# Reordering the early stage of a chunked-scan and gated-FFN kernel: weight groups of two, earlier loads, the decay matmul moved, D in two parts

## The chip, the cores and the metric

The kernel runs on one core of one Trainium2 chip. The metric is device time in us. A profiled execution gives a trace, with a span from its first to its last instruction; the span is some 1.7 to 2.0 us shorter than the time. Engines: TensorE (PE, its weight loads PEld), VectorE (DVE), ScalarE (ACT), GpSimd (POOL), SyncE (SP, which issues most of the DMAs here). In this kernel matmul results go to banks of PSUM, and another engine copies them out ("evacuates" them).

## The reference

```python
# x (4, 8, 768, 32), a (4, 8, 768), B and C (4, 8, 768, 16), float32
for each chunk of 32 tokens:                      # the kernel uses chunks of 64 or 128
    M = (C @ B^T) * decay(i, j) * causal          # C @ B^T is "G" in the kernel
    y = M @ x + (C @ state) * decay_to_i          # "D" and "inter" in the kernel
    state = decay_full * state + sum_j B x decay  # "state sums" (adds, carry, pass_on)
t = y as (3072, 256)
out = (relu(t @ w_gate) * (t @ w_val)) @ w_out    # 256 -> 1536 -> 256
```

## The kernel before

Batch 0 is worked off in pairs of 256 tokens (pairs 0 to 2), the FFN in blocks of 512 tokens. Each engine gets its instructions in the order of the program. From pair 3 on the scan is woven into the FFN, and that part is not changed. The pieces that matter:

```python
def keep_warm(n, tag="shared"):          # "dummies": results are never read
    ...
    for _ in range(n):
        nc.tensor.matmul(out=w, lhsT=warm, rhs=warm, start=True, stop=True)   # 128x128x128 bf16

def decay():                             # fp32, 64 rows; HC = 3, six records in the trace
    for k in range(HC):
        nc.tensor.matmul(out=d[:, k]..., lhsT=cp[:, k * 128:(k + 1) * 128], rhs=pick...)

def D_wide(p):                           # 32 small matmuls
    for t in range(2):
        for r in range(2):
            for i in range(2):
                ...
                for q in range(4):       # q: head group = column group of the array
                    nc.tensor.matmul(out=y[32 * q:32 * q + 32, t], lhsT=..., rhs=...,
                                     tile_position=(64 * i, 32 * q), ...)
...
keep_warm(20)
d = factors(); decays(0); decays(1)      # fp32 matmuls
keep_warm(3)
...
weights(0, 4)                            # GpSimd DMA, w_gate and w_val, four 128-column tiles each
...
scan(0, H)
scale_wide(1, 1, P_); weights(4, 8); scale_wide(1, 0, P_)      # pair 1, on GpSimd
keep_warm(4)
G_wide(0)
keep_warm(16)
...
cast_x(0, A_); adds(0)                   # state sums of pair 0
keep_warm(3)
...
pass_on(0, 0); carry(0, 0); middle(); inter_wide(0); D_wide(0)
turn(1, True); yevac_wide(0, A_, V); ...
f0 = gvh(0, 0, 0, True)                  # FFN, one tile of 128 columns, 256 tokens ("a half")
G_wide(1)
decay()
...
```

## Time and profile before

| | before |
|---|---|
| time, median of the first 3 runs | 130.36 us (130.0 to 130.37) |
| span of the profiled run | 129.2 us (a fourth run, time 130.95 us) |
| TensorE busy | 121.2 us, 94% |
| TensorE alone on the chain of waits | from 35.1 us on, but for the last copy (0.42 us) |
| holes of TensorE before that | 0.54 (at 10.96), 0.55 (15.55), 1.47 (25.28) |

"Busy" is the time in which an instruction's record runs. The profile's rows and timelines are shown in the prediction.

### The profile page before, as it was taken

What the parts mean: (1) busy time and instruction counts of PE and PEld (TensorE: products, weight loads), DVE (VectorE), ACT (ScalarE), POOL (GpSimd) and SP (SyncE); (2) the same over time, 40 slices, a digit from 0 to 9 for tenths busy, and PEclk for the clock granted to TensorE, in tenths of its full rate; (3) what the DMA queues carried; (4) which work ended last, traced back from release to release, by engine and by line L of the source; (5) the groups of instructions that cost most, each with busy time, mean ns of one, the idle gap of its engine ahead of it and who ended that gap; (6) DMA issues with size and microseconds to landing.
All of it is one profiled execution on the core that took longest, in us unless ns stands there. A gap on an engine that the chain in (4) does not pass through costs nothing.

```text
span 129.2 us, 3445 instructions
## 1 busy us (share of the span) xinstructions
PE 121.2 (94%) x1288; PEld 84.5 (65%) x1294; DVE 88.5 (68%) x201; ACT 81.7 (63%) x186; POOL 40.2 (31%) x84
## 2 busy tenths in 40 slices
PE   6998899599999999999999999999999999999990
PEld 6764577258677567784567875477864577854770
DVE  4895968436599966578675878765789675688410
ACT  0567579355588854787844797935887745876310
POOL 6558402477285003480003760011930033000000
PEclk9999999999999999999999999999999999999999
DMA  4999999998889987288841188932200002200031
GB/s 71 208 152 186 173 210 196 122 121 100 100 101 215 105 110 90 86 143 108 99 61 66 41 139 98 103 49 89 81 0 0 0 5 81 81 0 5 0 110 52
DMA packets 72208, 12.14 MB, mean 94 GB/s; under 512 B 65936, under 2 KB 72192, under 8 KB 72192
## 3 DMA queue, kind: packets, MB, share of 16 engines
q1 hardware_dynamic: 66096, 8.91, 44.2%
q0 software_dynamic: 3184, 2.36, 13.0%
q10 hardware_dynamic: 2912, 0.66, 2.4%
q8 instruction: 10, 0.16, 0.6%
q14 instruction: 6, 0.05, 0.1%
HBM read 11.13 MB, written 3.15 MB: 110 GB/s over the span
## 4 chain that ended last, share of the span: by engine, by line
PE 82%; DMA 9%; DVE 2%; issue 2%; ACT 2%; POOL 0%; SPq 0%; DVEq 0%; POOLq 0%; ACTq 0%
PE o L604 24%; PE gv L586 15%; PE val L571 13%; PE gate L568 12%; DMA bcr<-in_B_dram 9%; PE w L184 4%; PE y L543 2%; PE tp L325 2%; PE g L469 2%; PE A_ps L506 1%; PE y L532 1%; PE g L362 1%; DVE h L575 1%; PE tpb L325 1%; ACT CT L343 1%
## 5 line engine op out<-in xcount | busy, mean ns | idle before, releaser
L575 DVE TENSOR_TENSOR h<-r,val 128x512 bf16<-128x512 bf16 x42 | 28.3, 685 | 9.9 <-ACT r L574 8.9
L604 PE MATMUL o<-wo,h 128*128 128x256 bf16 x288 | 34.8, 273 | 0.1
L604 PEld LDWEIGHTS <-h 128*128 128x128 bf16 x288 | 27.4, 98 | 5.5 <-issue 1.3
L574 ACT ACTIVATE r<-gate 128x512 bf16<-128x512 f32 x42 | 24.6, 601 | 6.4 <-PE gate L568 5.0
L592 DVE TENSOR_TENSOR h<-r,gv 128x256 bf16<-128x256 bf16 x60 | 23.7, 419 | 7.0 <-ACT r L589 6.6
L477 POOL TENSOR_SCALAR_AFFINE_SELECT gs<-gs 128x512 bf16<-128x512 bf16 (+1 forms) x18 | 9.0, 523 | 52.5 <-ACT gs L488 52.5
L571 PE MATMUL val<-yT,wv 128*128 128x512 bf16 x84 | 25.0, 379 | 0.3
L589 ACT ACTIVATE r<-gv 128x256 bf16<-128x256 f32 x60 | 22.6, 384 | 3.6 <-PE gv L586 1.7
L568 PE MATMUL gate<-yT,wg 128*128 128x512 bf16 x78 | 23.7, 379 | 0.0
L586 PE MATMUL gv<-yT,wv 128*128 128x256 bf16 x120 | 22.9, 273 | 0.6 <-DMA wv<-in_moe_w_val_dram 0.5
L586 PE MATMUL gv<-yT,wg 128*128 128x256 bf16 x120 | 23.0, 273 | 0.2
L494 DVE TENSOR_TENSOR gs<-g,maskUT 128x512 bf16<-128x512 f32 x18 | 11.6, 686 | 10.4 <-issue 9.7
L571 PEld LDWEIGHTS <-wv 128*128 128x128 bf16 x84 | 8.2, 98 | 9.9
L586 PEld LDWEIGHTS <-wv 128*128 128x128 bf16 x120 | 11.6, 98 | 2.5 <-DMA wv<-in_moe_w_val_dram 1.2
L586 PEld LDWEIGHTS <-wg 128*128 128x128 bf16 x120 | 11.1, 98 | 2.3 <-issue 0.5
L568 PEld LDWEIGHTS <-wg 128*128 128x128 bf16 x84 | 7.8, 98 | 5.8
L295 POOL TENSOR_TENSOR bs<-bcr,scaleBC 128x256 bf16<-128x256 f32 x18 | 11.0, 633 | 0.7 <-DMA bcr<-in_C_dram 0.7
L488 ACT CAST gs<-g 128x512 bf16<-128x512 f32 x9 | 5.3, 589 | 7.0 <-PE g L469 7.0
L620 ACT COPY ob<-o 128x512 f32<-128x512 f32 x10 | 5.8, 584 | 4.7 <-PE o L604 4.7
L556 ACT CAST yT<-y 128x512 bf16<-128x512 f32 x9 | 5.3, 586 | 5.5 <-PE y L543 5.3
L184 PE MATMUL w<-warm 128*128 128x128 bf16 x49 | 6.2, 308 | 1.1 <-DVE tmask L155 1.1
L325 PEld LDWEIGHTS <-bs 128*128 128x128 bf16 x48 | 3.5, 99 | 5.1 <-POOL bs L281 2.3
(100 smaller groups left out, 119.4 us busy)
## 6 DMA issues: line engine op xcount, KB each, us to landing
out_dram<-ob SPq DMA_DIRECT2D x10, 256.0 KB, 2.2
xr<-in_x_dram SPq DMA_DIRECT2D x19, 128.0 KB, 3.6
bcr<-in_C_dram SPq DMA_DIRECT2D x19, 64.0 KB, 3.3
bcr<-in_B_dram SPq DMA_DIRECT2D x19, 64.0 KB, 3.4
wg<-in_moe_w_gate_dram POOLq DMA_DIRECT2D x3, 256.0 KB, 5.6
wv<-in_moe_w_val_dram POOLq DMA_DIRECT2D x3, 256.0 KB, 6.1
wo<-in_moe_w_out_dram POOLq DMA_DIRECT2D x1, 768.0 KB, 11.6
xr<-in_x_dram SPq DMA_DIRECT2D x2, 256.0 KB, 8.6
```

The lines of the kernel that those rows point to most:

```text
L184: nc.tensor.matmul(out=w, lhsT=warm, rhs=warm, start=True, stop=True)
L295: eng.tensor_tensor(out=bs.rearrange("s k (q t n) -> s k t q n", q=4, t=2)[:, :, t], in0=src[:, :, t], in1=f[:, :, 4 * t:4 * t + 4].to_bro ...
L477: nc.gpsimd.affine_select(out=dst, in_=dst, pattern=[[0, n], [1, 128]], compare_op=ALU.is_ge, fill=0.0, base=0, channel_multiplier=-1)
L494: nc.vector.tensor_tensor(out=d[:, q], in0=g[q], in1=m, op=ALU.mult)
L568: nc.tensor.matmul(out=g, lhsT=wg[:, k, fs], rhs=yT[:, k, tk], start=(k == 0), stop=(k == 1))
L571: nc.tensor.matmul(out=v, lhsT=wv[:, k, fs], rhs=yT[:, k, tk], start=(k == 0), stop=(k == 1))
L574: nc.scalar.activation(r, g, AF.Relu)
L575: nc.vector.tensor_tensor(out=fst[b][:, f], in0=r, in1=v, op=ALU.mult)
L586: nc.tensor.matmul(out=gv_[:, j], lhsT=w[:, k, fs], rhs=yT[:, k, tk], start=(k == 0), stop=(k == 1), skip_group_check=True)
L589: nc.scalar.activation(r, gv_[:, 0], AF.Relu)
L592: nc.vector.tensor_tensor(out=fst[b][:, f, u * 256:(u + 1) * 256], in0=r, in1=gv_[:, 1], op=ALU.mult)
L604: nc.tensor.matmul(out=o[:, ts % 2], lhsT=fst[b][:, f, ts * 128:(ts + 1) * 128], rhs=wo[:, f], start=(f == 0), stop=(f == NF - 1), skip_gr ...
```

## The change

The intent is to close the three holes and to get the decay matmul out of real work. Weights come in groups of two tiles; loads of pairs 1 and 2 are let go sooner; w_out comes in two halves, the second later; the decay matmul takes the place of dummies; D is split by head group so that only one group waits for the last mask; pair 1's evacuation comes sooner; one output copy is split over two engines.

```diff
-        nc.vector.tensor_scalar_mul(pick[:, 0], pairs[:, 0], rmid)
+        nc.gpsimd.tensor_scalar_mul(pick[:, 0], pairs[:, 0], rmid)
...
-    def D_wide(p):
+    def D_wide(p, qs=(0, 1, 2, 3)):
...
+        if b == 0 and ts == 3:
+            nc.scalar.copy(out=ob[:, 0], in_=fst["o"][:, 0])
+            nc.vector.tensor_copy(ob[:, 1], fst["o"][:, 1])
...
-    weights(0, 4)
+    weights(0, 2)
+    weights(2, 4)
...
     scan(0, H)
+    middle()
     scale_wide(1, 1, P_)
-    weights(4, 8)
+    weights(4, 6)
     scale_wide(1, 0, P_)
+    weights(6, 8)
     keep_warm(4)
     G_wide(0)
-    keep_warm(16)
+    keep_warm(7)
+    load_x(1, nc.sync)
...
+    decay()
+    keep_warm(3)
     cast_x(0, A_)
     adds(0)
-    keep_warm(3)
...
+    decay_factors()
     pass_on(0, 0)
     carry(0, 0)
-    middle()
+    D_wide(0, (2, 3, 0))
     inter_wide(0)
-    D_wide(0)
+    D_wide(0, (1,))
     turn(1, True)
     yevac_wide(0, A_, V)
+    load(2)
+    load(3)
     carry(0, 1)
+    cast_x(1, P_)
     weights(8, NF)
-    cast_x(1, P_)
-    weights_out(0, NF)
+    weights_out(0, NF // 2)
...                                   (pair 1: adds, carry, pass_on, D and yevac sooner,
...                                    FFN halves 4 and 5 after them; weights_out(NF // 2, NF)
...                                    after scale_wide(2, 1))
+    halves(0, 1, 0, 1, 2, 3)
+    halves(0, 0, 6, 7)
+    halves(0, 1, 4, 5, 6, 7)
     gv(0, 8)
+    carry(1, 1)
+    pass_on(1, 1)
```

More of the change, by code (lines that the diff above doesn't have):

```diff
@@ L448, in D_wide @@
                     y = s["yw"][i][:, 0:256].rearrange("s (t m) -> s t m", t=2)
-                    for q in range(4):
+                    for q in qs:
                         nc.tensor.matmul(
@@ L619, in foevac @@
             return
-        nc.scalar.copy(out=ob, in_=fst["o"])
+        if b == 0 and ts == 3:
+            nc.scalar.copy(out=ob[:, 0], in_=fst["o"][:, 0])
+            nc.vector.tensor_copy(ob[:, 1], fst["o"][:, 1])
+        else:
+            nc.scalar.copy(out=ob, in_=fst["o"])
         nc.sync.dma_start(
@@ L647 @@
     scan(0, H)
+    middle()
     scale_wide(1, 1, P_)
-    weights(4, 8)
+    weights(4, 6)
     scale_wide(1, 0, P_)
+    weights(6, 8)
     keep_warm(4)
     G_wide(0)
-    keep_warm(16)
+    keep_warm(7)
+    load_x(1, nc.sync)
     gcopy(0, 0)
     gmask(0, 2, V, True)
-    load_x(1, nc.sync)
     gcopy(0, 1)
+    decay()
+    keep_warm(3)
     cast_x(0, A_)
     adds(0)
-    keep_warm(3)
     gmask(0, 3, V, True)
@@ L679, in halves @@
             gvh(b, f, u)
-    load(2)
-    load(3)
     f0 = gvh(0, 0, 0, True)
     G_wide(1)
-    decay()
     gcopy(1, 0)
@@ L691 @@
     gmask(1, 3, V, True)
+    adds(1)
+    carry(1, 0)
+    pass_on(1, 0)
     late += [gvh(0, 2, 0, True)]
-    adds(1)
     gmask(1, 0, V)
     gmask(1, 1, V)
-    carry(1, 0)
-    late += [gvh(0, 3, 0, True), gvh(0, 4, 0, True)]
-    pass_on(1, 0)
-    late += [gvh(0, 5, 0, True)]
-    decay_factors()
+    late += [gvh(0, 3, 0, True)]
+    D_wide(1, (2, 3, 0))
     inter_wide(1)
-    D_wide(1)
+    D_wide(1, (1,))
+    yevac_wide(1, A_, A_)
+    late += [gvh(0, 4, 0, True), gvh(0, 5, 0, True)]
     for fin in late:
@@ L705 @@
     nc.vector.reciprocal(wfac[:, 0, :, :, 2], wfac[:, 1, :, :, 2])
-    yevac_wide(1, A_, A_)
-    halves(0, 0, 6, 7)
-    carry(1, 1)
-    pass_on(1, 1)
     load(4)
@@ L712 @@
     scale_wide(2, 1, P_)
+    weights_out(NF // 2, NF)
     scale_wide(2, 0, P_)
@@ L720 @@
         nc.gpsimd.tensor_scalar_mul(smask[:, t], bd, tmask[:, t:t + 1])
-    halves(0, 1, 0, 1, 2, 3, 4, 5, 6, 7)
+    halves(0, 1, 0, 1, 2, 3)
+    halves(0, 0, 6, 7)
+    halves(0, 1, 4, 5, 6, 7)
     gv(0, 8)
+    carry(1, 1)
+    pass_on(1, 1)
     gv(0, 9)
```

## The prediction

Times per packet in it are means over the packet records of the kernel before. The 0.60 us for 128x128 is one of GpSimd's two multiplies with tmask in that run (26.63, 1.20 us for both).

> **What bounds the kernel now.** I read the page first: the engine shares, the slices, the chain of waits.
>
> ```profile
> PE 121.2 (94%) x1288; PEld 84.5 (65%) x1294; DVE 88.5 (68%) x201; ACT 81.7 (63%) x186; POOL 40.2 (31%) x84
> PE   6998899599999999999999999999999999999990
> DMA  4999999998889987288841188932200002200031
> PE 82%; DMA 9%; DVE 2%; issue 2%; ACT 2%; POOL 0%; SPq 0%; DVEq 0%; POOLq 0%; ACTq 0%
> ```
>
> TensorE is busy 94% of the span. Only slices 1, 4, 5 and 8 are thin, all before 29 us. From 35.1 us the chain is TensorE alone, so whatever reaches that point sooner ends sooner by the same amount. The DMA row says that the 16 DMA engines are full for the first nine slices; that is the other suspect for the early stage.
>
> Next, the TensorE timeline from 0 to 50 us, for the holes (the bracket is idle time, and what ended it):
>
> ```profile
> 10.96 0.29 PE L325 MATMUL tpb<-ident,bs 128*128 128x128 bf16 x2 [0.54 <-DVE T L415]
> ...
> 12.20 0.88 PE L248 MATMUL dec<-pick,cp 64*128 64x64 f32 x6
> 13.01 0.39 PE L586 MATMUL gv<-yT,wg 128*128 128x256 bf16 x2
> ...
> 15.55 0.39 PE L586 MATMUL gv<-yT,wv 128*128 128x256 bf16 x2 [0.55 <-DMA wv<-in_moe_w_val_dram]
> ...
> 25.28 0.29 PE L325 MATMUL tp<-ident,bs 128*128 128x128 bf16 x2 [1.47 <-POOL bs L281]
> ```
>
> The holes are 0.54, 0.55 and 1.47 us, 2.56 in all. The change aims at all three and at the decay matmuls (0.88). Then the timelines of the other engines and the chain, for what stands behind each hole:
>
> ```profile
> 12.32 1.07 ACT L379 CAST gs<-g 128x512 bf16<-128x512 f32 x2
> 8.61 0.76 POOL L193 DMA_DIRECT2D wg<-in_moe_w_gate_dram  x1
> 9.37 0.73 POOL L193 DMA_DIRECT2D wv<-in_moe_w_val_dram  x1
> 10.10 0.80 POOL L281 TENSOR_TENSOR bs<-bcr,wfac 128x128 bf16<-128x128 f32 x2
> 24.44 0.78 POOL L281 TENSOR_TENSOR bs<-bcr,wfac 128x128 bf16<-128x128 f32 x2 [3.61 <-DMA bcr<-in_B_dram]
> 11.51 0.06 DVE L84 MEMSET bcr<- 1x1 f32 x1
> 12.04 12.27 DMA bcr<-in_B_dram
> ```
>
> Hole 1 is charged to DVE, but the GpSimd scaling of pair 1's B ends at 10.90, 0.06 before TensorE goes on. It stands behind two weight issues of 1.5 us on the GpSimd queue, and I take it for the true releaser. Hole 2 is a 4-tile weight group that has not landed. Hole 3 is pair 2's B: its load is held back by a one-element DVE memset at 11.51, goes out at 12.04 and takes 12.27 us for 128 KB, while 64 KB loads later take a median of 3.4.
>
> [...]in the packet records a weight packet takes some 114 ns and a w_out packet 60, a small packet of pair 2 13; C and B crawl exactly while weights and w_out flow (until 24.8 us). [...]the bytes are not fewer after the change, only in another order. [...]the trace has 0.60 for 128x128 there, so I put the pick at 0.3.
>
> **The change, part by part.**
>
> *Decay matmul among the dummies.* Now it takes TensorE from 12.20 to 13.01, after G of pair 1. But the next FFN matmul needs a PSUM bank, freed by the first ScalarE copy of G: two take 1.07 us from 12.32, so the first ends near 12.9. Without decay TensorE waits until about 12.95. Worth 0.06, not 0.88. In its new place it replaces 9 of 16 dummies (1.0 us); three more dummies move from after the state sums to before them.
>
> *pick on GpSimd.* GpSimd now issues four weight DMAs first: 4.56 + 0.93 + 0.72 + 0.76 + 0.73 = 7.70, then the pick until 8.0. The seven dummies end at 7.75, so decay runs 8.05 to 8.9, three dummies to 9.2, the state sums end near 9.45 instead of 9.02. The two decay_factors copies (0.38) slip in before the state copy on ScalarE. That is a loss of 0.3 to 0.4.
>
> *D in two parts.* After the state copy only inter (0.29) and 8 of 32 D matmuls remain instead of all 32 (0.34). Gains 0.25 to 0.35. yT of pair 0 ends near 10.7 as now. Sum so far: 0.
>
> *Hole 1.* GpSimd: pick to 8.0, scale C to 8.8, two issues to 10.3, scale B to 11.1. So the transpose starts at about 11.15 instead of 10.96. But the first FFN matmul's weights have by then landed (w_val reached it at 11.52 now, 0.34 of weight-load wait), so G of pair 1 starts at 11.85 as now. Sum: 0 ± 0.2.
>
> *13 to 17.2 us.* The stretch holds five FFN halves (0.44 each), the state sums 0.2, inter 0.55, D 0.34: 3.3 of 4.2 us. Tiles 4 and 5 move behind D and come in their own group, issued by 10.3, so hole 2 should go. carry and state of pair 1 now follow the third mask. From the durations: masks end at about 14.9 on DVE, the state copy at 14.6 on ScalarE, D's last part at 15.3, yT of pair 1 at 16.0, and FFN halves 4 and 5 cover the wait. The next half starts near 16.2 instead of 17.22: gain 1.0.
>
> *16 to 23 us.* Ten halves (10 x 0.437) and gv 8 and 9 (2 x 0.86) are the same work. They end near 22.35 instead of 23.5. Weights 8 to 12 are issued at 13.2 to 14.7 instead of 10.8 to 12.3. Now they land by some 18.5, and they are needed at 20.6; I expect no wait.
>
> *Hole 3.* The memset goes to about 10.8 (0.7 sooner), and pair 2's loads stand ahead of weights 8 to 12 and all of w_out; the weights ahead of them are in packets half as long. B should land at 17 to 20.5, is needed by 21.5. Gain 1.47.
>
> *w_out in two halves.* The second half is issued when C of pair 2 is scaled, at 16 to 18. All of w_out lands at 24.8 now, and the total of DMA work is unchanged, so it lands at 25 to 26. TensorE then reaches the second half's tiles at 24.3 + 0.7 = 25.0. Cost 0 to 1.0, expected 0.4.
>
> *Pair 3.* Its last C lands around 29 now, its scaling takes 1.38 on GpSimd (31.05 to 32.43), and TensorE asks for it at 32.72. With TensorE 2.4 sooner, loads that are bound by total bytes give 30.4 against 30.3. Cost 0 to 0.5, expected 0.2.
>
> *Two-engine output copy.* The hole before the FFN at 35.1 is 0.13 (34.97 to 35.10). Gain 0.1. The rest of that matmul stage is untouched.
>
> Sum: 0.06 + 1.0 + 1.47 + 0.1 = 2.6 gained, 0.6 returned in new waits: 2.0 of 130.36, so 128.35.
>
> **Rivals.**
> 1. *The wait moves to w_out or weights 8 to 12.* For it: the DMA row is full until 29 us and the same bytes must come through in 2.5 us less. Against: q0 has some slack, as wo is only needed at its end. It would return 1 to 1.5 us: 129.2 to 129.8.
> 2. *All holes close and nothing takes their place.* For it: needed-by times that I computed have 1 to 2 us of margin except for w_out's second half and pair 3. It gives 130.36 - 2.6 to 2.9 = 127.5 to 127.8.
> 3. *The early stage slips.* The pick behind four GpSimd issues delays decay, the state sums and pair 1's scaling, by 0.5 or more where I have 0.2. For it: the GpSimd queue is tight from 4.56 to 12. Against: the pick is only 64x32. Result 128.7 to 129.
> 4. *Decay's whole 0.88 is won.* Against: the bank wait behind it. It would make rival 2 about 127.
>
> **Range and chances.** Centre 128.3. Rival 2 or 4 alone crosses 2% (127.75 or less), about one chance in four. Slower needs 2.6 us of new waits on top of all gains; the part of the kernel after 35 us has none of the changed work, so it is unlikely. 8 in 10: 127.5 to 129.5.
>
> **What would show each step.** Right: decay at 8 to 9 us and still an idle stretch or bank wait of some 0.7 before the second FFN half at about 13; no hole on DMA w_val near 15; no or little hole before pair 2's second transpose, now near 22.5, with B's landing under 10 us; the FFN of block 1 beginning near 33 instead of 35.1. Wrong: a TensorE hole at the first w_out matmuls (rival 1) or a transpose of pair 1 after 11.4 (rival 3); DMA waits after 40 us that reach TensorE. If the second FFN half starts at 12.3 rather than 13, rival 4 is right.

## The result, and the profile after

The changed kernel took 133.92 us (median of 4 runs, 133.43 to 134.49), the kernel before 130.37 beside it (130.0, 130.36, 130.37 and a slow run of 132.70). Ratios here are the mean time of one kernel's fast runs over that of the other's of the same rounds, so not quite the ratio of the medians. The ratio is 1.028, with an interval of 1.022 to 1.034: slower by almost 3%, where I had predicted a gain of 1.6%.

The page of the changed kernel, the same rows as before (engine shares, slices of TensorE and DMA, the chain):

```profile
PE 125.0 (94%) x1285; PEld 86.2 (65%) x1285; DVE 89.1 (67%) x201; ACT 82.2 (62%) x186; POOL 43.9 (33%) x90
PE   6997799998989999999999999999999999999990
PEclk9999999999999999999999999999999999999999
PE 87%; POOL 3%; ACT 2%; DVE 2%; issue 2%; DMA 2%; DVEq 0%; ACTq 0%
```

DMA has gone from 9% to 2% of the chain: hole 3 is closed, as meant. But TensorE is busy 3.8 us longer with the same FFN and scan work and nine dummies fewer. So the same work ran slower. The timeline of TensorE shows where (start, length, instructions, count, idle before):

```profile
7.01 0.93 PE L184 MATMUL w<-warm 128*128 128x128 bf16 x7
8.18 1.53 PE L248 MATMUL dec<-pick,cp 64*128 64x64 f32 x6 [0.23 <-POOL pick L240]
9.64 0.50 PE L184 MATMUL w<-warm 128*128 128x128 bf16 x3
...
15.37 0.59 PE L586 MATMUL gv<-yT,wg 128*128 128x256 bf16 x2 [0.69 <-ACT gs L379]
...
16.56 0.61 PE L586 MATMUL gv<-yT,wg 128*128 128x256 bf16 x2
16.96 0.64 PE L586 MATMUL gv<-yT,wv 128*128 128x256 bf16 x2
17.39 0.63 PE L586 MATMUL gv<-yT,wg 128*128 128x256 bf16 x2
...
19.94 0.39 PE L586 MATMUL gv<-yT,wg 128*128 128x256 bf16 x2
20.17 0.38 PE L586 MATMUL gv<-yT,wv 128*128 128x256 bf16 x2
20.39 0.38 PE L586 MATMUL gv<-yT,wg 128*128 128x256 bf16 x2
...
26.92 0.39 PE L325 MATMUL tp<-ident,bs 128*128 128x128 bf16 x4
```

Look at the starts. Each FFN line is two matmuls of 256 columns. Before 19.8 us these pairs follow each other every 0.38 to 0.43 us; from 19.94 on every 0.22 to 0.23, which is the rate of the kernel before already at 13 us (13.01, 13.24, 13.46). The decay matmuls (six records) take 1.53 us instead of 0.88. TensorE ran at half rate.

The kernel before shows the same half rate, but only in its first microseconds:

```profile
6.38 0.65 PE L362 MATMUL g<-CT,BT 32*64 32x256 bf16 x16
6.96 1.89 PE L184 MATMUL w<-warm 128*128 128x128 bf16 x16
...
11.85 0.42 PE L362 MATMUL g<-CT,BT 32*64 32x256 bf16 x16
```

The same 16 matmuls of G take 0.65 us for pair 0 and 0.42 for pair 1. This stood in the trace that I had before I predicted.

The trace holds clock records that the page hardly shows: until the first record the PEclk row counts the clock as full (the records stand in the packed trace; no view prints their times). Counted from the start of the span, the first record that grants the full clock lies at 9.15 us in the kernel before and at 19.80 us in the changed one. Until then the starts show half rate in both. And the dummies are no filler: with nine fewer, as the only edit, the time rose by 1.0% and the profiled run was without the full clock again from 11.44 to 18.26 us (b_dummies7). Below, the clock "opens" where a record of the full clock starts, and "closes" where it ends.

The records of a run also keep one step. The full clock lasts 119.466 us in the kernel before and 112.640 in the changed one, 35 and 33 times 3.413 us. Where it was lost and regained in one run (b_loads) the records lie at 8.05, 11.47 and 18.29 us, one and two times 3.413 apart. The starts of the dummies agree with the records: 0.107 us apart before and 0.056 after (the variant a_decay_back, record at 7.73). I call a stretch of 3.413 us, counted from a run's clock records, a window.

GpSimd's timeline after the change, for holes 1 and 3:

```profile
7.71 0.41 POOL L240 TENSOR_SCALAR pick<-identf,rmid 64x32 f32<-64x32 f32 x1
10.30 0.79 POOL L281 TENSOR_TENSOR bs<-bcr,wfac 128x128 bf16<-128x128 f32 x2
18.30 0.78 POOL L281 TENSOR_TENSOR bs<-bcr,wfac 128x128 bf16<-128x128 f32 x2 [2.83 <-DMA bcr<-in_C_dram]
22.17 0.78 POOL L281 TENSOR_TENSOR bs<-bcr,wfac 128x128 bf16<-128x128 f32 x2 [2.26 <-DVE wfac L714]
```

The pick came when I had said. Pair 2's B (22.17) now waits for a DVE reciprocal and not for its load. The plan of the change worked here, while TensorE was at half rate. But each weight DMA took 0.72 to 0.78 us of GpSimd's time (the first 0.93) with 128 KB as with 256 KB, in both kernels, so halving the groups doubled that time for the same bytes.

### The profile page after: what moved, and what is told of

Read it like the earlier page. It is cut to its first block, busy times and chain, and to the rows that moved or that the text cites.

```text
span 132.3 us, 3437 instructions
## 1 busy us (share of the span) xinstructions
PE 125.0 (94%) x1285; PEld 86.2 (65%) x1285; DVE 89.1 (67%) x201; ACT 82.2 (62%) x186; POOL 43.9 (33%) x90
## 3 DMA queue, kind: packets, MB, share of 16 engines
q1 hardware_dynamic: 66096, 8.91, 44.4%
## 4 chain that ended last, share of the span: by engine, by line
PE 87%; POOL 3%; ACT 2%; DVE 2%; issue 2%; DMA 2%; DVEq 0%; ACTq 0%
PE o L604 24%; PE gv L586 22%; PE gate L568 13%; PE val L571 13%; PE y L543 2%; PE tp L325 2%; PE g L469 2%; PE y L450 2%; DMA a<-in_a_dram 2%; PE A_ps L506 1%; PE y L532 1%; POOL wg L193 1%; PE dec L248 1%; POOL wv L193 1%; PE g L362 1%
## 5 line engine op out<-in xcount | busy, mean ns | idle before, releaser
L592 DVE TENSOR_TENSOR h<-r,gv 128x256 bf16<-128x256 bf16 x60 | 24.4, 418 | 7.3 <-ACT r L589 6.6
L568 PE MATMUL gate<-yT,wg 128*128 128x512 bf16 x84 | 25.0, 379 | 0.0
L586 PE MATMUL gv<-yT,wg 128*128 128x256 bf16 x120 | 23.8, 282 | 1.2 <-ACT gs L379 0.7
L586 PE MATMUL gv<-yT,wv 128*128 128x256 bf16 x120 | 23.9, 282 | 0.0
L571 PEld LDWEIGHTS <-wv 128*128 128x128 bf16 x84 | 8.2, 98 | 10.0 <-issue 0.2
L586 PEld LDWEIGHTS <-wv 128*128 128x128 bf16 x120 | 12.2, 101 | 1.8
L624 ACT COPY ob<-o 128x512 f32<-128x512 f32 x9 | 5.2, 583 | 3.8 <-PE o L604 3.8
L184 PE MATMUL w<-warm 128*128 128x128 bf16 x40 | 5.4, 311 | 1.1 <-DVE tmask L155 1.1
L514 DVE TENSOR_TENSOR Sm<-A_ps,smask 128x256 bf16<-128x256 f32 x15 | 6.2, 412 | 0.0
## 6 DMA issues: line engine op xcount, KB each, us to landing
xr<-in_x_dram SPq DMA_DIRECT2D x19, 128.0 KB, 3.5
wg<-in_moe_w_gate_dram POOLq DMA_DIRECT2D x4, 128.0 KB, 3.6
wv<-in_moe_w_val_dram POOLq DMA_DIRECT2D x4, 128.0 KB, 3.8
```

The costliest lines, as they stand in the source:

```text
L514: nc.vector.tensor_tensor(out=n, in0=acc["A"], in1=smask, op=ALU.mult)
L568: nc.tensor.matmul(out=g, lhsT=wg[:, k, fs], rhs=yT[:, k, tk], start=(k == 0), stop=(k == 1))
L571: nc.tensor.matmul(out=v, lhsT=wv[:, k, fs], rhs=yT[:, k, tk], start=(k == 0), stop=(k == 1))
L586: nc.tensor.matmul(out=gv_[:, j], lhsT=w[:, k, fs], rhs=yT[:, k, tk], start=(k == 0), stop=(k == 1), skip_group_check=True)
L592: nc.vector.tensor_tensor(out=fst[b][:, f, u * 256:(u + 1) * 256], in0=r, in1=gv_[:, 1], op=ALU.mult)
```

## The experiments

Twelve runs, each beside the kernel before. The runs of one kernel differ: the kernel before alone spread over 129.1 to 131.7 in 52 runs. The clock has a part in such spreads, as the profiled runs of b_loads (lost again, 131.9) and a_dummies16 (opened at 20.25, 134.54) show, but its part was not shown run by run. The labels (slow above 1.5% over the same kernel's fastest) also mark these two runs, and a ratio of fast runs flatters a kernel that has a few lucky runs. In the changed kernel the loss shows in its fast runs, all four.

The record lists the mean granted clock of each run, in which the time before the first clock record counts as full. The two profiled runs that lost the clock again for two windows (b_dummies7, b_loads) have 0.974, which is 1 less half of 6.83 us over a span of 130. I take 0.974 as the mark of such a run also where no trace was kept. A run that opens late is not told apart by this number (the changed kernel's profiled run, opened at 19.80, shows 1.0).

My theory: the moved decay and the missing dummies, over 6 to 12 us, are why the clock opens ten microseconds late (19.80 against 9.15). The rival: the new order itself has a fixed wait (loads, pair 1, GpSimd). A later question was why, with the clock right, the predicted gain still did not come.

### a_again: the changed kernel once more

No edit.

> The changed kernel once more, unedited, for the spread. Clock theory[...]: nearly all runs at 133 to 135, opening at 16 to 21 us; a run that opens early would be at 130 to 131. Rival (the loss is a fixed wait in the new order): all runs within 0.5 us of each other.

Measured: 132.0 to 134.12, mean 133.53 over 6 runs; the profiled run opened at 19.35 us. The ratio over its fast runs is 1.019 (1.011 to 1.026). The record marks the two slowest (134.03, 134.12) slow, so this ratio is on the low side, and its verdict is "unclear" at 2%. No run came near 130, so the loss holds in another set of runs; and one run at 132.0 against the rest at 133.5 and more speaks against a wait of fixed size.

### b_dummies7: the kernel before with fewer dummies

```diff
-    keep_warm(16)
+    keep_warm(7)
```

> The kernel before with one number changed: 7 dummies instead of 16 after G of pair 0. Clock theory[...]: the clock record opens at 12 us or later instead of near 9, the FFN halves of 256 columns run at some 0.2 us each until then, and the time is 132.5 to 134.5. Rival (the loss comes from the waits that the new order makes, dummies are only filler): within 0.3 us of before, 130 to 130.6.

Measured: 131.55 median, ratio 1.010 (1.004 to 1.016). A clear loss from taking out nine results that nobody reads; the rival falls. But it is well under half of what I expected, and the course was a little different: in the profiled run the clock opened early, at 8.02, closed again at 11.44 and reopened at 18.26. TensorE was recorded busy for only 1.77 us of that closing window.

### b_decay_early: the decay part alone

```diff
-        nc.vector.tensor_scalar_mul(pick[:, 0], pairs[:, 0], rmid)
+        nc.gpsimd.tensor_scalar_mul(pick[:, 0], pairs[:, 0], rmid)
-    keep_warm(16)
+    keep_warm(7)
...
+    decay()
+    keep_warm(3)
     cast_x(0, A_)
     adds(0)
-    keep_warm(3)
...                  (decay_factors before pass_on(0, 0); middle after scan; the old places empty)
```

> The kernel before with the decay part of the change alone (pick on GpSimd, decay and 3 dummies after 7 dummies, none after the state sums, its evacuation before the first state copy). Clock theory: opens late as in the changed kernel, 132.5 to 135. Rival (loss from loads and pair 1's order): 129.8 to 130.8.

Measured: 132.12 median, four runs within 131.90 to 132.43; ratio 1.014 (1.008 to 1.019); opens at 20.22 us. It loses half of what the whole change loses, and is under the range that I gave. The trace says why: pair 2's transposes start at 26.54 us instead of 23.53, but without the hole of 1.47 us that follows there in the kernel before. The late B load covered that much of the lost clock. The full change had closed that hole, so its clock loss is paid in full.

### b_fp32_dummies: as long, but fp32

```diff
-    keep_warm(16)
+    keep_warm(3)
+    keep_warm_f32(6)        # 64x64 fp32 matmuls of identf with identf
```

The question: with TensorE at work as long, does it matter for the clock that the work is fp32? The rival says no.

> The kernel before, its 16 bf16 dummies after G of pair 0 replaced by 3 bf16 ones and 6 fp32 matmuls of 64x64, about as long in time (no new wait, no decay moved). [...]the decay matmul in that place costs the clock: opens near 18 to 20 us in most runs, 132 to 135. Rival[...]: opens at 7.5 to 10, 129.5 to 131 as before.

Measured: 131.9 median, ratio 1.011 (1.006 to 1.016); opens at 19.27 us. The size is again under what I expected, but the rival falls. In the window 5.62 to 9.03 TensorE is recorded busy for 3.32 of 3.41 us, and the clock does not open; in the kernel before, with 3.38 us in the window 5.74 to 9.15 and bf16 dummies, it opens. So here fp32 matmuls of 64x64 did not make up for bf16 dummies. Nor is idle time needed: in b_decay_early the window 6.57 to 9.98 was recorded busy throughout, 1.54 us of it decay, and did not open the clock.

All fourteen profiled runs fit this when they are cut into windows of 3.413 us, counted from their clock records (the records of one run lie whole windows apart, up to 35, as in the kernel before). Twenty windows at half clock were recorded busy for 3.26 us or more and held 0.95 us or more of fp32 matmuls, six of them starting after 5.6 us; the clock opened at the end of none. The sixteen windows at whose end it opened were busy for 3.24 to 3.41 us and held at most 0.19 us of fp32. Small bf16 tiles did not prevent it: the changed kernel's window before the opening (16.39 to 19.80) holds 1.66 us of matmuls of 64x32 and 32x32. So in the place of nine dummies stands the decay matmul, and the clock opened at the end of no window that held it whole. What exactly decides, the runs do not show: one window (b_fp32_dummies, 9.03 to 12.44), busy for 3.24 us with 0.11 us of fp32, had no opening at its end either, and bf16 dummies of 64x64 were not tried.

### a_dummies16: the changed kernel with its dummies back

```diff
-    keep_warm(7)
+    keep_warm(16)
```

> The changed kernel with 16 dummies again after G of pair 0, all else as changed (decay follows the dummies). Clock theory: the clock opens near 9 to 9.6 us, the loss goes and the holes that the change closes show: 128.0 to 130.0. Rival (the decay matmul and the pick wait in front of the state sums are the loss): the state sums are later still, time 133.5 to 135.

Measured: six runs in two groups, 130.23, 130.57, 130.65 and 133.47, 134.54, 134.79; nothing between. The ratio of 1.000 (0.992 to 1.009) is over the three fast ones. The profiled run is one of the slow group and opened at 20.25 us: its window 6.59 to 10.01 was recorded busy throughout, with 1.2 us of it decay. So the dummies alone take the loss away in half of the runs, short of the 128.0 to 130.0 that I expected. Of the slow half only this run's windows are seen. The run at 133.47 has a granted clock of 0.974, the mark of a clock that opened early and was lost again.

### a_decay_back: decay at its old place

```diff
-    keep_warm(7)
+    keep_warm(16)
-    decay()
-    keep_warm(3)
     cast_x(0, A_)
     adds(0)
+    keep_warm(3)
-    decay_factors()
     pass_on(0, 0)
...
     G_wide(1)
+    decay()
...
     pass_on(1, 0)
+    decay_factors()
```

> The changed kernel with decay and its evacuation back at their old places and all dummies as before (16 and 3); weight groups, earlier loads, D in two parts and the new order of pair 1 kept. Clock theory: opens near 9.2 us as before, and my prediction's other terms hold: 127.7 to 129.2. Rival (the new order of pair 1 or of the loads is the loss): 132 or more.

Measured: 130.46 median, 130.19 to 130.84, ratio 1.001 (0.995 to 1.007); opens at 7.73. The 3.5 us are gone with this, and loads and pair 1's order, which this variant keeps, are cleared of the loss. But my other terms were to give 2 us, and the timed runs show none. The TensorE timeline of the profiled run, the fastest of the four:

```profile
9.56 0.23 PE L450 MATMUL y<-gs,xb 64*32 64x128 bf16 x3 [0.32 <-ACT T L413]
...
9.90 0.29 PE L436 MATMUL Aps<-CT,Sw 32*32 32x128 bf16 x8
10.12 0.23 PE L450 MATMUL y<-gs,xb 64*32 64x128 bf16 x1
...
10.45 0.29 PE L325 MATMUL tp<-ident,bs 128*128 128x128 bf16 x2
11.40 0.29 PE L325 MATMUL tpb<-ident,bs 128*128 128x128 bf16 x2 [0.66 <-POOL bs L281]
...
25.45 1.77 PE L604 MATMUL o<-wo,h 128*128 128x256 bf16 x11
27.54 0.28 PE L604 MATMUL o<-wo,h 128*128 128x256 bf16 x1 [0.32 <-DVE h L575]
...
34.30 0.38 PE L586 MATMUL gv<-yT,wg 128*128 128x256 bf16 x2 [0.38 <-DVE ob L622]
```

There are four things to see. D's first part waits for the last ScalarE copy out of the same bank (9.56), so it gains nothing by standing first. Second, these 24 matmuls take 0.34 us (9.56 to 9.90), and the last 8, all of one head group, take 0.33 (10.12 to 10.45), as long as all 32 took whole (9.79 to 10.14 before). Third, the first w_out row takes from 25.45 to 27.75, where 12 such matmuls take some 1.4 alone. Fourth, the split output copy makes the FFN wait 0.38 us where it had waited 0.13.

Behind the third is ScalarE (its timeline):

```profile
23.84 0.35 ACT L424 ACTIVATE Sw<-T,dec 128x64 bf16<-128x64 f32 x1 [1.42 <-DVE T L415]
24.09 0.57 ACT L574 ACTIVATE r<-gate 128x512 bf16<-128x512 f32 x1
24.57 0.36 ACT L340 COPY BT<-tp 128x256 bf16<-128x256 bf16 x1
24.82 0.85 ACT L343 ACTIVATE CT<-tp,tmask 128x256 bf16<-128x256 bf16 x2
25.55 1.10 ACT L574 ACTIVATE r<-gate 128x512 bf16<-128x512 f32 x2
```

The state copy (pass_on) was moved in front of the relu of tile 9 and waits 1.42 us for DVE; then the three copies of pair 2's transposes stand in front of the last two relus. As long as hole 3 was open, this work was hidden in it.

### b_dsplit: D in two parts alone

```diff
-    inter_wide(0)
-    D_wide(0)
+    D_wide(0, (2, 3, 0))
+    inter_wide(0)
+    D_wide(0, (1,))
...                  (the same for pair 1)
```

> The kernel before with D in two parts by head group as the only edit. Theory from the trace of the variant with decay put back: 8 matmuls of one head group all use one column group of the array and take 0.33 us, as long as 32 spread over four, so the split costs 0.3 us for each of pairs 0 and 1 unless a wait hides it: 130.4 to 131.2. Rival (my prediction's term: the split saves 0.25 to 0.35 after the state copy): 129.8 to 130.3. The verdict rests on the profile's D and inter times.

Measured: mean 130.35 over 20 runs, before 130.32 over 52; ratio 1.000 (0.997 to 1.003). In its profile the last 8 matmuls run from 10.16 to 10.49, 0.33 us, as I had read. But the time does not change: in this kernel a wait hides it (the next transpose comes at 11.10 whatever D does). The reading was right and its price was not. In these traces 8 matmuls of one column group take as long as 32 spread over four (0.33 us against 0.35 in the kernel before), and the split takes 0.34 and 0.33 us where D whole took 0.35.

### a_fix: the waits of a_decay_back mended

```diff
-    D_wide(0, (2, 3, 0))
     inter_wide(0)
-    D_wide(0, (1,))
+    D_wide(0)                       (the same for pair 1)
-        if b == 0 and ts == 3: ...  (output copy whole again)
     yevac_wide(1, A_, A_)
+    carry(1, 1)
...
+    halves(0, 1, 0, 1)
+    pass_on(1, 1)
...
-    tevac(2, A_, A_)
+    tevac(2, A_, V)
```

> The variant with decay put back, and also D whole again, the output copy whole again, the second carry of pair 1 straight after its evacuation and its state copy two halves later, CT of pair 2 on DVE instead of ScalarE. Theory (these are the waits that ate the gain: D 0.3 x 2, output copy 0.3, ScalarE in front of the last relus 0.6 to 0.9): 128.6 to 129.6. Rival (the gain is lost to DMA): 130 to 131.

Measured: 129.58 median over 17 runs, ratio 0.995 (0.992 to 0.998). The gain is real but small. The three slowest runs (131.49 to 131.98) have a granted clock of 0.974, the mark of a clock lost again. The TensorE timeline shows the next limit:

```profile
25.04 0.82 PE L604 MATMUL o<-wo,h 128*128 128x256 bf16 x6
26.53 0.81 PE L604 MATMUL o<-wo,h 128*128 128x256 bf16 x6 [0.67 <-DMA wo<-in_moe_w_out_dram]
```

The relus are in time now, and the second half of w_out is not. The DMA row of this run's page is at 9 until 25.5 us; this is rival 1 of my prediction, with 0.67 us.

The stage in numbers, from the timelines of four profiled runs (us from the start of the span):

| | before | changed | a_decay_back | a_fix |
|---|---|---|---|---|
| full clock granted | 9.15 | 19.80 | 7.73 | 9.86 |
| state sums of pair 0 | 8.78 | 10.08 | 8.71 | 8.91 |
| G of pair 1 | 11.85 | 14.04 | 12.07 | 11.90 |
| first FFN half after halves 0 to 5 | 17.22 | 20.82 | 16.82 | 16.93 |
| transposes of pair 2, second one | 25.28 | about 27.0 | about 23.2 | about 23.2 |
| G of pair 2 | 28.79 | 31.55 | 27.75 | 27.27 |
| FFN of block 1 | 35.10 | 38.11 | 34.30 | 33.59 |
| span | 129.2 | 132.3 | 128.5 | 127.7 |

The columns are single runs whose clock opened at different times, so differences of some tenths between them are not the edit's alone. From the row of block 1 to the end all four take 94.1 to 94.2 us: what is lost or gained at 35 us is lost or gained at the end.

### a_fix_pool: hole 1 as well

```diff
     scan(0, H)
-    middle()
     scale_wide(1, 1, P_)
-    weights(4, 6)
     scale_wide(1, 0, P_)
-    weights(6, 8)
+    middle()
+    weights(4, 6)
...
     cast_x(1, P_)
+    weights(6, 8)
```

> As the one before, and GpSimd scales both halves of pair 1 before it issues the third weight group (hole 1). Theory: the pair-1 transpose starts near 10.5 instead of 11.4, G of pair 1 some 0.6 earlier: 128.0 to 129.2, 0.4 to 0.8 under the one before. Rival (the third weight group then lands too late for FFN halves 4 and 5): a hole on DMA wv near 15.5, same time as the one before.

Measured: 129.90 median over 20 runs, ratio 0.998 (0.995 to 1.000), no better than a_fix. The transpose did start at 10.54, but the first FFN half then started at 11.18 and G at 11.71 (0.37 us of wait, put down to DVE), and later tiles waited for weights: TensorE waits 0.52 us on w_val at 19.59, so FFN starts that a_fix has at 19.13 came at 19.82, and again 0.19 us at 22.78. The edit moved the fourth weight group too, behind the cast of pair 1's x, which the expectation leaves out. This is a miss; the weight groups were moved too late.

### b_loads: the load part alone

```diff
-    weights(0, 4)
+    weights(0, 2)
+    weights(2, 4)
...                  (weights(4, 8) in two, x of pair 1, loads of pairs 2 and 3 sooner,
...                   w_out in two halves, all as in the change)
```

> The kernel before with the load part of the change alone: weights in groups of two, x of pair 1 and pair 2 sooner, w_out in two halves. My prediction's terms for it: holes at 15 and 23.8 us close (0.55 + 1.47) less 0.4 for w_out, so 128.7 to 129.3 against 130.1. Rival (the DMA engines are full until 29 us, so the wait moves to the second half of w_out): 129.6 to 130.4, with a hole on DMA wo at the first w_out matmuls.

Measured: 22 runs from 128.73 to 131.93, in groups: seven at 128.7 to 129.6, eight at 129.7 to 131.0, and seven at 131.6 to 131.9. The ratio of the fast runs is 0.992 (0.989 to 0.996); the mean of all runs, 130.30, is only 0.26 under before. The profiled run is of the slow group. In it the clock opens at 8.05, closes at 11.47 and comes back at 18.29, and TensorE has this wait in the closing window:

```profile
11.41 0.38 PE L325 MATMUL tpb<-ident,bs 128*128 128x128 bf16 x2 [1.10 <-POOL bs L281]
```

GpSimd scaled pair 1 later. Its C started at 8.17 instead of 7.88, after 0.53 us of waiting for the load (the four weight issues had ended at 7.64), and took 0.95 us instead of 0.77; B, behind two weight issues as before, started at 10.57 instead of 10.10. So hole 1 grew from 0.54 to 1.10, and the window was busy for 1.91 of 3.41 us. In a_decay_back a window with 2.35 us (7.73 to 11.14) did not close the clock. Why C landed later was not tested. Six of the seven slow runs have a granted clock of 0.974, so I count them as the profiled one, with the clock lost; the seventh (131.63) has 1.0. The other 16 runs have a mean of 129.74, against 130.50 for the 44 runs of before without 0.974: earlier loads are worth some 0.8 us where the clock holds, and in these runs, by that count, it was lost more often (6 of 22 against 3 of 47). No wait on w_out shows in the profiled run, but this run is late and proves nothing for a fast one.

### b_warm and a_fix_warm: more dummies

```diff
     adds(0)
-    keep_warm(3)
+    keep_warm(5)
...
-    turn(1, True)
+    transp(1, 1, True)
+    keep_warm(5)
+    transp(1, 0, True)
```

> The kernel before with 7 more dummies and no other edit: 5 instead of 3 after the state sums, 5 between the two transposes of pair 1, where TensorE waits. Clock theory: [...]the runs at 131.4 to 131.7[...] become fewer: mean 0.2 to 0.6 us under before. Rival (dummies are filler and only cost time): 0 to 0.4 us over before.

> The repaired variant (decay at its old place, D whole, output copy whole, ScalarE order mended) with the same 7 dummies more. Clock theory: its three runs of 17 near 131.5 to 132 go, the rest unchanged: 129.0 to 129.6, ratio to before 0.990 to 0.996. Rival: as without them or slower.

Measured for b_warm: 129.10 to 131.22 over 22 runs, mean 130.26 against 130.56 of before; ratio 0.998 (0.996 to 1.001). Not clear of noise, but seven more useless matmuls cost nothing that these runs show, and the highest run fell from 131.63 to 131.22. For a_fix_warm: 128.67 to 130.50, all ten runs fast, ratio 0.991 (0.987 to 0.995). The three runs of a_fix near 131.5 to 132 have no counterpart, and no run of b_warm or a_fix_warm has 0.974. That is too few runs to show that the dummies did it: at a_fix's share, 3 of 17, ten runs without one come about one time in seven. This version beats both kernels: 129.58 us median against 130.50 of before in the same rounds.

## Why the prediction was wrong, point by point

- **Decay among the dummies (predicted 0 for the early stage): the step that failed.** I wrote that decay "replaces 9 of 16 dummies (1.0 us)", as if a dummy were worth the time it takes. With nine gone and fp32 in their place the clock opened at 19.80 instead of 9.15, and G of pair 1 started at 14.04 where I had 11.85. a_decay_back, b_decay_early and b_fp32_dummies show it. The same step had a second error: I took decay's 0.85 us from a stretch at full clock (12.20) and moved it to 8.05, where even the kernel before has half rate (full clock from 9.15). It took 1.53 us, which is most of why the state sums started at 10.08 where I had 9.2. None of my rivals contained either.
- **Decay hidden behind the bank wait: right.** Without decay the next FFN half waits 0.69 us for ScalarE's copy of G (at 15.37). Rival 4 falls.
- **Pick on GpSimd (8.0): right,** 7.71 to 8.12.
- **D in two parts (0.25 to 0.35 gained): wrong in sign on TensorE.** It costs 0.3 us there, and nothing in the time (b_dsplit).
- **Hole 1 (11.15): a little later,** 11.40 in a_decay_back, at the edge of rival 3's sign. In the changed kernel GpSimd kept my times (B scaled from 10.30 to 11.09), and the hole is covered by the slow clock.
- **13 to 17 us (gain 1.0): 0.3 to 0.4 in the profiled runs,** 17.22 to 16.82 in a_decay_back and 16.93 in a_fix. Hole 2 did close.
- **Hole 3 (gain 1.47): closed,** but a part came back at once: ScalarE's order in front of the last relus. I had counted that hole as if only TensorE had work in it.
- **w_out's second half (0.4 expected): 0.67 in a_fix,** where the relus no longer wait in front of it.
- **Output copy (gain 0.1): cost 0.25.** The two engines copy one after the other out of the bank (0.37 and 0.42 us in a row), against 0.59 for one copy.
- **The rest untouched: right,** 94.1 to 94.2 us in four variants.

With the clock put right, the terms sum to 0.8 us at the FFN of block 1 (35.10 to 34.30) and not to 2.0. Even that flatters them: the profiled run of before took 130.95 us with the clock from 9.15, the one of a_decay_back 130.19 with the clock from 7.73, and over the timed runs the ratio is 1.001. So a predicted time of 128.3 would have been too low even then.

## What to carry to other kernels

Before you treat instructions as filler, run the kernel with fewer of them (here nine fewer cost 1.0%, b_dummies7); find the matmul rate in the starts of equal instructions in the timeline, and not in the busy share. In this kernel fp32 matmuls (b_fp32_dummies, 1.011; b_decay_early, 1.014) or a longer wait (b_loads, 1.10 us) came with a full clock that was late, or lost, until 18.3 to 20.2 us in the profiled runs. That cost more than their own length: 1.1% with dummies as long but fp32, and in b_loads, where the wait had grown by 0.56 us, seven slow runs at 131.6 to 131.9 against a mean of 129.74 for the others. When a hole on the bounding engine closes, look for the work that was hiding in it on the others.
